# Attention scores with each head's block of q in its own quarter of the TensorE array

## The chip, the cores and the metric

One core of one Trainium2 chip. The metric is the device time of one execution, in microseconds; the median of the runs counts. The engines are called PE (TensorE matmuls; PEld its weight loads), DVE (VectorE), ACT (ScalarE), POOL (GpSimd) and SP (SyncE, which issues the transfers).

## The reference, cut to what matters

Attention for 2 batches of 8 heads, 768 positions, 64 values per head, float32. Every query sees the keys less than 16 positions away and, for each block of 32 positions, one pooled key (the maximum over the block) with a pooled value (the mean).

```
k_sum = k.reshape(B, H, nb, block, D).max(axis=3)
v_sum = v.reshape(B, H, nb, block, D).mean(axis=3)
scores_l = scale * np.matmul(q, k.transpose(0, 1, 3, 2))
mask_l = np.abs(pos[:, None] - pos[None, :]) < window
scores_s = scale * np.einsum('bhsd,bhnd->bhsn', q, k_sum) + np.log(block)
a = softmax(concatenate([where(mask_l, scores_l, -1e9), scores_s], -1))
out = np.matmul(a, np.concatenate([v, v_sum], axis=2))
```

The result, 1536 tokens of 512 values, goes through a mixture of 8 experts (router by argmax, 512 to 1024 to 512) and a dense feed-forward layer (512 to 2048 to 512, squared relu).

## The kernel before, in words

The heads are worked in 8 pairs (4 pairs for each batch); a pair's two heads lie one above the other on the 128 partitions, 64 each. A pair's 768 queries are 12 tiles of 64. For a tile, 96 keys around it and the 24 pooled keys, 120 in all, stand beside one another in `kt`. The array's stationary operand was built as a block-diagonal 128 x 128 matrix in `qb`: q of head 0 (64 x 64) in the upper left, q of head 1 in the lower right, zeros elsewhere. One matmul of `qb` with `kt` (128 x 120) so gives 128 rows of scores, 64 for each head. In float32 each matmul is two passes on PE, each with its weight load (96 matmuls stand as 192 in the profile).

Tiles go in groups of four (`groups`: 23 of four tiles and 2 of two at the end), and one iteration of the main loop (L569) issues a stage of several groups, so that each engine has its part of another group: `do_t(i-2)` transposes the weights of the group before the last (L383) and ACT copies them (L385); `do_s(i)` makes scores (L360) into a tile `ps` of one PSUM bank, and DVE adds the mask and takes the maximum (L366); `do_o(i-3)` multiplies with v (L401), DVE divides (L407); `prep(i+2)` lays out keys (POOL, L282), pooled keys (L284) and q (L287), mostly on ACT, for two groups ahead; `do_x(i-4)` transposes the result (L429); `do_l(i-5)` multiplies with the router's weights (L448); `do_e(i)` takes exp on ACT (L375). The order of all engines' instructions is that of the program text.

At every third iteration a new pair of heads begins. Then SP issues, one after another: the spreading of the pooled values into `vw` (`put_vsum`, L317), which waits for the small transfer `vt` (`vmean`, L314), and behind it the loads of k, q and v for pairs to come (L260, L261, L291, L294). `vmean(n+1)` is issued two iterations later, then `store_x` (L420). SP is one queue in order of issue.

At the end of the stage the first expert's weights are loaded, tokens are sorted by expert, and 13 slots of 128 tokens go through the experts; then comes the dense layer. These use hi and lo parts in float32r, three matmuls for each product. The change doesn't touch them.

Of the kernel before, what the change touches and what calls it, by code (L numbers as in the profile page):

```python
# [11 lines left out]
F32 = mybir.dt.float32  # L12
# [14 lines left out]
P = 128  # L27
NT = S // 64
# [12 lines left out]

# columns of the float32 constants
C_ID = 0
# [43 lines left out]
def tile_kernel(ctx: ExitStack, tc: tile.TileContext, a, out, dbg=None):  # L87
    nc = tc.nc
    ctx.enter_context(tc.manual_schedule())

    # ---- pools that live through the kernel
    cp = ctx.enter_context(tc.tile_pool(name="const", bufs=1))
# [17 lines left out]

    # ---- moe2 weights: float64 bits to float32
    pend, todo = [], [(j, c) for j in range(NF) for c in range(2)]
# [44 lines left out]

    # ---- a slot of 128 tokens of one expert
    def gather(s, x=None, rows=N):
# [59 lines left out]

    # ================= attention =================  # L220
    rt = ctx.enter_context(tc.tile_pool(name="route", bufs=1))
# [4 lines left out]
    with ExitStack() as ax:  # L226
# [14 lines left out]
        kts = [kq.tile([P, NT, NK], F32, name=f"kt{i}") for i in range(2)]  # L241
        qbs = [kq.tile([P, NT, P], F32, name=f"qb{i}") for i in range(2)]
        vws = [wk.tile([NK, NT, 129], F32, name=f"vw{i}", bufs=1) for i in range(3)]
        nc.gpsimd.memset(qbs[0], 0.0)
        for t in vws:
# [17 lines left out]
        STARTK = {0:nc.vector.tensor_copy,1:nc.vector.tensor_copy}  # L263
        STARTQ = {0:nc.vector.tensor_copy}

# [10 lines left out]
        def prep(i):  # L276
            n, t0, c = groups[i]
            kp, qp = kqs[n]
            kt, qb = kts[n % 2][:, t0:t0 + c], qbs[n % 2]
            w = kp[:, 64 * t0:64 * t0 + 96]  # L280
            w = bass.AP(w.tensor, w.offset, [list(w.ap[0]), [64, c], [1, 96]])
            nc.gpsimd.tensor_copy(kt[:, :, NB:], w)  # L282
            ek, *eq = (STARTK.get(i, nc.scalar.copy), STARTQ.get(i, nc.scalar.copy), nc.scalar.copy)
            ek(kt[:, :, 0:NB], kss[n].unsqueeze(1).broadcast_to([P, c, NB]))  # L284
            for h in range(2):
                r = slice(64 * h, 64 * h + 64)
                eq[h](qb[r, t0:t0 + c, r], qp[r, 64 * t0:64 * t0 + 64 * c].rearrange("p (t q) -> p t q", q=64))  # L287

# [6 lines left out]

        # means of v over the blocks: [block, quarter of the columns] on the partitions, then [block]
        def vsum(n, lo=0, hi=32):
# [22 lines left out]
        groups = [(n, t, 4) for n in range(8) for t in (0, 4, 8)][:-1] + [(7, 8, 2), (7, 10, 2)]  # L320
        # the tensor engine gets to its full clock
        zw = kq.tile([P, P], F32, name="zw")
        nc.vector.memset(zw, 0.0)
        nc.vector.memset(qbs[1], 0.0)
        warm = kq.tile([1, 1], F32, name="warm")
# [6 lines left out]
        kp, qp = kqs[0]  # L332
# [21 lines left out]
        def do_s(i):  # L354
            n, t0, c = groups[i]
            kt, qb = kts[n % 2], qbs[n % 2]
            pb = ps_s.tile([P, 512], F32, name="ps", tag="ps")
            ps = pb[:, 0:c * NK].rearrange("p (c k) -> p c k", k=NK)
            for u in range(c):
                nc.tensor.matmul(ps[:, u], qb[:, t0 + u], kt[:, t0 + u], start=True, stop=True)  # L360
            spare[i] = pb[:, 4 * NK:]
            sm = wk.tile([P, c, NK], F32, name="sm", tag="sm")
            mx = wk.tile([P, c], F32, name="mx", tag="mx")
            # the negated scaled scores, and the least of them
            for u in range(c):
                nc.vector.tensor_tensor_reduce(sm[:, u], ps[:, u], msk[:, (t0 + u > 0) + (t0 + u == NT - 1)], -0.125, 3e38,  # L366
                                               op0=ALU.add, op1=ALU.min, accum_out=mx[:, u:u + 1])
            sp[i] = sm, mx
# [94 lines left out]
        mxl = rt.tile([P, NTILE], F32, name="mxl")  # L463
        # of every token: experts as [taken | later than the taken], expert-major
        oh = rt.tile([P, B, 2, E, 6], F16, name="oh")
# [20 lines left out]

        # The first token's expert comes first. Its weights are loaded ahead, and its first 128 tokens
        # of the first batch are gathered before the second batch is through: beside column sums of
        # the scores (iterations 18 to 21).
        def first_slot(i, x):  # L490
# [7 lines left out]
            elif i == 20:  # L498
                mine = rsh[:, 0, 0, 0:1]
                nc.tensor.matmul(x[:, 0:1], ones, csh[:, C_NEG:C_NEG + 1], start=True, stop=False)  # L500
                nc.tensor.matmul(x[:, 0:1], tri, mine, start=False, stop=True)
                nc.tensor.matmul(x[:, 1:2], ones, mine, start=True, stop=True)

                def after():
                    r6 = vb.tile([P, 6], F16, name="r6", bufs=1)
                    nc.vector.tensor_scalar(r6, cum[:, 0, 0], x[:, 0:1], None, op0=ALU.add)
                    # what the first slot lacks, and where the second one begins
                    nc.vector.tensor_scalar(few, x[0:1, 1:2], P - 0.5, None, op0=ALU.is_lt)
                    nc.vector.tensor_scalar(row1, x[0:1, 1:2], float(P), None, op0=ALU.min)
                    nc.vector.tensor_scalar(lack[:, E:E + 1], x[0:1, 1:2], -float(P), 0.0, op0=ALU.add, op1=ALU.min)  # L510
                    nc.vector.tensor_scalar(lack[:, 0:1], lack[:, E:E + 1], -1.0, None, op0=ALU.mult)
                    nc.vector.tensor_tensor(t6, tok[:, 0:6], oh[:, 0, 0, 0], op=ALU.mult)
                    nc.vector.tensor_tensor(a6, io12[:, :, 0:6], r6.unsqueeze(1).broadcast_to([P, P, 6]), op=ALU.is_equal)
            elif i == 21:
                for d in range(6):
                    nc.tensor.matmul(x[:, 0:1], a6[:, :, d], t6[:, d:d + 1], start=d == 0, stop=d == 5)

                def after():
                    ixs[0] = rt.tile([P, 1], I32, name="ix0")
                    nc.vector.tensor_copy(ixs[0], x[:, 0:1])  # L520
                    gather(0, wk.tile([P, DM], F32, name="xg0", bufs=1), S)
            else:
                return None
# [173 lines left out]

    # ================= routing =================
    yp0 = ctx.enter_context(tc.tile_pool(name="yp0", bufs=1, **tiled))
# [20 lines left out]
    with ExitStack() as rx:  # L720
# [23 lines left out]

        # position of every token in the order by expert
        for b in range(B):
# [30 lines left out]
        nc.vector.tensor_scalar(nf, cb[:, 0:1], P + 0.5, None, op0=ALU.is_lt)  # L777
        # the second slot begins with the 129th token in the order, if the first slot is a full one
        ixs[1] = order_i[:, 1:2]
# [10 lines left out]
    def tables():  # L790
        s5 = [1, NREG, E]
        # slots of 128 tokens of one expert: expert of each
        ci = rg.tile([1, E], I32, name="ci")
# [10 lines left out]
        nc.vector.tensor_scalar(ec, er, float(E - 1), None, op0=ALU.min)  # L804
        # as it is numbered outside
        eo_ = rg.tile([1, NREG], F32, name="eo_")
# [5 lines left out]
        yield  # L812
        # first row of each slot; what lies past the last one goes to rows of its own
        off = rg.tile([1, E], F32, name="off")
# [11 lines left out]

        # gate of every token
        ex = rg.tile([P, NTILE, E], F32, name="ex")
# [15 lines left out]
    def w_split(j):  # L844
        wh = whs[j] = st.tile([P, 1024], F32R, name="st4", tag="st4") if j < 2 else w2p.tile([P, 1024], F32R, name=f"wh{j}", tag=f"wh{j}")
        nc.scalar.copy(wh, wf[j])
        # it takes the place of a chunk that is already split
        wl = wls[j] = wf_tile(F32R) if j <= NF else \
            w2p.tile([P, 1024], F32R, name="wf", tag="wf", bufs=NCH - NF)
        nc.vector.tensor_tensor(wl, wf[j], wh.bitcast(F32), op=ALU.subtract)  # L850

    # ================= mixture of experts =================
    with mx_:
# [76 lines left out]

        # dense rows that the first 11 and 12 slots have filled for good, however the tokens are spread:
        # at most 8 of them are not full
        def y_first_load(t):
# [65 lines left out]

    # ================= second feed-forward =================  # L1000
    with ExitStack() as fx:
# [8 lines left out]
        NI = NW * NCH  # L1010
        # relu(g a)^2 = g^2 relu(a)^2 as every gate is positive
        gd = yp.tile([P, NTILE], F32, name="gd")
# [23 lines left out]
        def z_mm(i):  # L1036
# [13 lines left out]
            if i == NI - LAST:  # L1050
                # the other window's tiles are read no more
                gh, gl = (t[:, 0] for t in yt1)
# [56 lines left out]
def lay_out(q, k, v, moe_modality_id, moe_w_gate, moe_modality_bias, moe_w1, moe_w2, moe2_w_in, moe2_w_out):  # L1109
    """The arrays as the program takes them: the inputs' own values, moved and padded."""  # L1110
    hp = H // 2
# [51 lines left out]
```

## Time and profile before

| | |
|---|---|
| runs | 569.95, 573.24, 574.92 us; median 573.24 |
| profiled execution | span 569.4 us from the first to the last instruction; its own time is not recorded apart, the lowest run is 0.5 us above the span |
| PE busy | 533.9 us (94%), 2676 matmul passes |
| PEld busy | 442.1 us (78%), 2676 weight loads |
| DVE, ACT, POOL busy | 293.1, 223.6, 100.7 us |
| granted PE clock | mean 0.972 of full |
| attention | about the first 105 us |

A busy engine is not an engine at its peak: matmuls are pipelined, and one instruction's duration is its latency, so the cost of a pass is read from the distance between starts. Idle time of an engine counts only where it is the one that the next step waits for.

### The profile page before, as it was taken

To read this page: it belongs to the slowest core of one execution; us is meant where nothing else is said; L and a number is where in the kernel's file an instruction comes from. 1 tells how busy PE (TensorE), PEld (TensorE's weight loads), DVE (VectorE), ACT (ScalarE), POOL (GpSimd) and SP (SyncE) were. 2 spreads that over 40 slices of the span, in tenths; PEclk is the share of its full clock that TensorE was granted. 3 is DMA by queue.
4 is the path that set the end of the run, shared out by engine and by line. 5 is a ranking of instruction groups with operands and counts; after the bars stand their busy time and mean duration, and the time that the engine had idled before them with its cause. 6 is when DMAs were issued, how large, how long until landed. Compare 5 with 4: busy or idle time off the path is not lost. (4 is left out here: it accounts for less than half of the span.)

```text
span 569.4 us, 8409 instructions
## 1 busy us (share of the span) xinstructions
PE 533.9 (94%) x2676; PEld 442.1 (78%) x2676; DVE 293.1 (51%) x836; ACT 223.6 (39%) x454; POOL 100.7 (18%) x115
## 2 busy tenths in 40 slices
PE   7795987979999999999889999999999999999995
PEld 6795976858878688888678888888888888888884
DVE  5885898571646953444968886423223223222230
ACT  5975886522225422223653445223222223221220
POOL 3333444640111500000317000002000000200002
PEclk8988899888999999999999999999999999999998
DMA  7795978603668644448519010001000000100001
GB/s 218 194 258 130 240 195 259 202 20 112 133 183 309 211 147 142 137 134 272 209 45 335 17 37 18 20 0 39 37 1 0 1 1 20 55 1 0 1 18 55
DMA packets 39829, 62.72 MB, mean 110 GB/s; under 512 B 19586, under 2 KB 22446, under 8 KB 39770
## 3 DMA queue, kind: packets, MB, share of 16 engines
q1 hardware_dynamic: 37386, 55.48, 32.6%
q0 software_dynamic: 2384, 6.56, 3.5%
q8 instruction: 23, 0.38, 0.3%
q14 instruction: 36, 0.29, 0.2%
HBM read 51.09 MB, written 9.71 MB: 107 GB/s over the span
## 5 line engine op out<-in xcount | busy, mean ns | idle before, releaser
L1049 DVE TENSOR_TENSOR g<-r 128x512 f32<-128x512 f32 x48 | 33.2, 691 | 106.0 <-ACT r L1047 106.0
L1047 ACT ACTIVATE r<-pz 128x512 f32<-128x512 f32 x48 | 28.7, 597 | 111.4 <-PE pz L1045 111.4
L1071 PE MATMUL pu<-wf,gh 128*128 128x512 f32 x180 | 70.5, 392 | 0.0
L1072 PE MATMUL pu<-wh,gl 128*128 128x512 f32 x156 | 61.6, 395 | 0.0
L1070 PE MATMUL pu<-wh,gh 128*128 128x512 f32 x156 | 61.5, 394 | 0.0
L1080 POOL DMA_INDIRECT out<-o,order_i x12 | 11.7, 976 | 236.8 <-DVE o L1079 215.4
L1044 PE MATMUL pz<-yt0h,wf 128*128 128x512 f32 x128 | 50.5, 395 | 0.0
L1058 ACT CAST gh<-g 128x512 fp32r<-128x512 f32 x45 | 28.0, 621 | 54.4 <-DVE g L1049 50.0
L1059 DVE TENSOR_TENSOR gl<-g,gh 128x512 fp32r<-128x512 f32 x45 | 31.2, 693 | 30.9 <-ACT gh L1058 28.9
L1043 PE MATMUL pz<-yt0h,wh 128*128 128x512 f32 x112 | 44.5, 397 | 0.0
L401 PE MATMUL po<-vw,pts 120*128 120x129 f32 x192 | 29.7, 297 | 15.4 <-DMA vw<-vt 10.8
L1045 PE MATMUL pz<-yt0l,wh 128*128 128x512 f32 x112 | 43.7, 390 | 0.0
L204 DVE TENSOR_TENSOR hl<-pt,hh 128x512 fp32r<-128x512 f32 x24 | 16.6, 690 | 47.7 <-ACTq L712 30.6
L177 PE MATMUL py<-w2l,hh 128*128 128x512 f32 x96 | 38.2, 398 | 2.9 <-DVE w2l L165 2.6
L178 PE MATMUL py<-w2h,hl 128*128 128x512 f32 x96 | 38.5, 401 | 1.6 <-DVE hl L204 1.4
L1071 PEld LDWEIGHTS pu<-wf,gh 128*128 128x128 f32 x180 | 33.8, 188 | 8.0
L401 PEld LDWEIGHTS po<-vw,pts 120*128 120x128 f32 x192 | 26.0, 206 | 17.8 <-issue 8.5
L176 PE MATMUL py<-w2h,hh 128*128 128x512 f32 x96 | 39.2, 409 | 0.0
L176 PE MATMUL ph<-w1h,xh 128*128 128x512 f32 x96 | 38.9, 405 | 0.0
L177 PE MATMUL ph<-w1l,xh 128*128 128x512 f32 x96 | 38.1, 397 | 0.0
L178 PE MATMUL ph<-w1h,xl 128*128 128x512 f32 x96 | 37.9, 395 | 0.0
L1072 PEld LDWEIGHTS pu<-wh,gl 128*128 128x128 f32 x156 | 29.3, 188 | 7.0
(239 smaller groups left out, 1129.5 us busy)
## 6 DMA issues: line engine op xcount, KB each, us to landing
st<-in_w SPq DMA_DIRECT2D x24, 512.0 KB
rw<-in_w SPq DMA_DIRECT2D x16, 512.0 KB
wf<-in_w SPq DMA_DIRECT2D x8, 512.0 KB
wh<-in_w SPq DMA_DIRECT2D x8, 512.0 KB
vw<-in_vw SPq DMA_DIRECT2D x7, 580.5 KB
y_dram<-ys SPq DMA_DIRECT2D x13, 256.0 KB
vk<-in_vk SPq DMA_DIRECT2D x8, 384.0 KB
wf<-in_kt SPq DMA_DIRECT2D x7, 400.0 KB
```

Source lines behind the costliest of these rows:

```text
L176: nc.tensor.matmul(ps, ah, bh, start=first, stop=False)
L177: nc.tensor.matmul(ps, ah, bl, start=False, stop=False)
L178: nc.tensor.matmul(ps, al, bh, start=False, stop=last)
L401: nc.tensor.matmul(po[-1][:, v, 0:129], pts[:, u + v], vw[:, t0 + u + v], start=True, stop=True)
L1043: nc.tensor.matmul(pz, wh[:, c], yh[:, k], start=k == 0, stop=False)
L1044: nc.tensor.matmul(pz, wl[:, c], yh[:, k], start=False, stop=False)
L1045: nc.tensor.matmul(pz, wh[:, c], yl[:, k], start=False, stop=k == 3)
L1049: nc.vector.tensor_tensor(g, r, r, op=ALU.mult)
L1059: nc.vector.tensor_tensor(gl, g, gh.bitcast(F32), op=ALU.subtract)
L1070: nc.tensor.matmul(acc[t], gh[:, c], wh, start=j == 0, stop=False)
L1071: nc.tensor.matmul(acc[t], gh[:, c], wl, start=False, stop=False)
L1072: nc.tensor.matmul(acc[t], gl[:, c], wh, start=False, stop=j == NCH - 1)
```

## The change

`qb` goes: its two buffers, their two memsets and the copies in `prep`. `do_s` takes q where the transfer has put it. Head h's 64 x 64 block of q is loaded as the stationary operand into the rows 64h to 64h+63 and the columns 64h to 64h+63 of the array, and multiplies only that head's half of `kt`. A tile's scores come from two matmuls where there was one; they land in the same places of the same PSUM tile.

```
-        qbs = [kq.tile([P, NT, P], F32, name=f"qb{i}") for i in range(2)]
-        nc.gpsimd.memset(qbs[0], 0.0)
...
-        STARTQ = {0:nc.vector.tensor_copy}
...
         def prep(i):
             n, t0, c = groups[i]
-            kp, qp = kqs[n]
-            kt, qb = kts[n % 2][:, t0:t0 + c], qbs[n % 2]
+            kp = kqs[n][0]
+            kt = kts[n % 2][:, t0:t0 + c]
...
-            ek, *eq = (STARTK.get(i, nc.scalar.copy), STARTQ.get(i, nc.scalar.copy), nc.scalar.copy)
+            ek = STARTK.get(i, nc.scalar.copy)
             ek(kt[:, :, 0:NB], kss[n].unsqueeze(1).broadcast_to([P, c, NB]))
-            for h in range(2):
-                r = slice(64 * h, 64 * h + 64)
-                eq[h](qb[r, t0:t0 + c, r], qp[r, 64 * t0:64 * t0 + 64 * c].rearrange("p (t q) -> p t q", q=64))
...
-        nc.vector.memset(qbs[1], 0.0)
...
         def do_s(i):
             n, t0, c = groups[i]
-            kt, qb = kts[n % 2], qbs[n % 2]
+            kt, qp = kts[n % 2], kqs[n][1]
             pb = ps_s.tile([P, 512], F32, name="ps", tag="ps")
             ps = pb[:, 0:c * NK].rearrange("p (c k) -> p c k", k=NK)
             for u in range(c):
-                nc.tensor.matmul(ps[:, u], qb[:, t0 + u], kt[:, t0 + u], start=True, stop=True)
+                for h in range(2):
+                    r = slice(64 * h, 64 * h + 64)
+                    nc.tensor.matmul(ps[r, u], qp[r, 64 * (t0 + u):64 * (t0 + u) + 64], kt[r, t0 + u], start=True, stop=True)
```

## Rows read from the trace of the kernel before

**Rows 1.** The page: busy tenths of PE in 40 slices of the span.

```profile
PE   7795987979999999999889999999999999999995
```

**Rows 2.** Windows: busy us (and instructions) of each engine in 20 us stretches.

```profile
core 0: us, PE busy (x) PEld busy (x) DVE busy (x) ACT busy (x) POOL busy (x), PEclk, DMA share, GB/s
...
40.00:60.00 20.00, 14.23 (x101) 13.82 (x101) 11.60 (x63) 12.14 (x37) 5.73 (x10) 0.83 0.66 165
60.00:80.00 20.00, 19.04 (x167) 18.50 (x167) 17.66 (x106) 17.23 (x52) 7.46 (x15) 1.00 0.86 234
```

**Rows 3.** Timeline, one dense group: start, length in all, what, how many.

```profile
65.10 1.05 PE L360 MATMUL ps<-kt,qb 128*128 128x120 f32 x8
...
65.99 1.06 PE L401 MATMUL po<-vw,pts 120*128 120x129 f32 x8
...
66.30 0.56 ACT L385 COPY pts<-pt 120x512 f32<-120x512 f32 x1
...
67.11 0.51 PE L448 MATMUL pl<-wg,xt 128*128 128x16 f32 x4
...
67.94 1.05 PE L360 MATMUL ps<-kt,qb 128*128 128x120 f32 x8
...
69.34 0.56 ACT L385 COPY pts<-pt 120x512 f32<-120x512 f32 x1
```

**Rows 4.** Waits of PE and PEld, 14 to 97 us: total us, times, longest.

```profile
PE po L401 <- DMA vw<-vt: 8.1, 4, 5.5
...
PEld po L401 <- ACT p L375: 4.6, 6, 1.6
PEld po L401 <- ACT qb L287: 2.6, 2, 1.9
```

**Rows 5.** Timeline of SP's transfers, and of PE at the stage's end.

```profile
34.38 0.84 SPq L317 DMA_DIRECT2D vw<-vt  x1
...
39.85 0.83 SPq L314 DMA_DIRECT2D vt<-vs  x1
...
50.64 0.84 SPq L317 DMA_DIRECT2D vw<-vt  x1
...
96.85 0.84 SPq L317 DMA_DIRECT2D vw<-vt  x1
...
100.28 1.41 PE L401 MATMUL po<-vw,pts 120*128 120x129 f32 x8 [2.65 <-DMA vw<-vt]
```

**Rows 6.** Groups by line and shape: busy us, mean ns, idle before.

```profile
L287 ACT COPY qb<-wf 64x256 f32<-64x256 f32 x45 | 18.1, 403 | 6.1 <-DMA wf<-in_qt 5.8
...
L448 PEld LDWEIGHTS pl<-wg,xt 128*64 128x64 f32 x8 | 0.6, 136 | 0.6 <-issue 0.6
```

**Rows 7.** Timeline, the second group at the start.

```profile
8.46 0.82 ACT L287 COPY qb<-wf 64x256 f32<-64x256 f32 x2 [2.83 <-DMA wf<-in_qt]
...
11.45 0.28 DVE L366 CUSTOM_DVE_ANT_0 sm<-ps,cst 128x120 f32<-128x120 f32 x1 [1.44 <-PE ps L360]
```

**Rows 8.** Timeline of PE and PEld, router products with whole and half weights.

```profile
108.63 0.27 PE L429 MATMUL px<-cst,xo 128*128 128x128 f32 x1
...
109.65 0.39 PE L178 MATMUL pt<-w1h,xl 128*128 128x512 f32 x1
109.88 0.27 PE L429 MATMUL px<-cst,xo 128*128 128x128 f32 x1
...
110.99 0.39 PE L178 MATMUL pt<-w1h,xl 128*128 128x512 f32 x1
...
108.63 0.53 PEld L448 LDWEIGHTS pl<-wg,xt 128*128 128x128 f32 x4
...
110.08 0.31 PEld L448 LDWEIGHTS pl<-wg,xt 128*64 128x64 f32 x4 [0.28 <-issue]
```

**Rows 9.** Timeline of PE around the 12-row matmul L451.

```profile
60.98 0.52 PE L448 MATMUL pl<-wg,xt 128*128 128x16 f32 x4
61.43 0.42 PE L451 MATMUL pl<-mb,m 12*128 12x48 f32 x2
...
62.26 1.05 PE L360 MATMUL ps<-kt,qb 128*128 128x120 f32 x8
```

## The prediction

> **What bounds the kernel now.** First the page's slices: TensorE (PE) is near full from slice 11 on and gappy only in the first seven or eight, which are the attention stage [rows 1]. Behind that stage PE runs without gaps, so I take it that a shift of the end of attention shows one for one at the end of the kernel. Next the windows: between 60 and 80 us PE works 19.04 of 20 us and ScalarE (ACT) 17.23, between 40 and 60 us PE only 14.23 [rows 2]. So the stage has two faces, dense groups and groups that wait.
>
> The timeline of one dense group shows the first. Scores start at 65.10 and again at 67.94: 2.84 us per group of four tiles. The eight score passes take 65.10 to 65.99, 0.111 us each. ACT meanwhile runs from one copy of the transposed weights to the next, 66.30 to 69.34, that is 3.04 us, without a gap [rows 3]. PE and ACT are both at their limit there, ACT a little over.
>
> The list of waits shows the second face. From 14 to 97 us the product with v (L401) waits 8.1 us for the DMA that spreads the block means of v, and its weight loads wait 4.6 us for exp and 2.6 us for the qb copies on ACT [rows 4]. The first of these belongs to a loop on the DMA queue: the means of head pair n+1 leave at L314 behind the bulk loads that follow L317 of pair n, and L317 of pair n+1 waits until they land. The one issued at 39.85 let L317 go at 50.64; four pairs later L317 is at 96.85, so a head pair there takes (96.85 - 50.64)/4 = 11.55 us, against 3 x 2.84 = 8.52 us of dense PE work. The last of them is what L401 waits for at 100.28, the end of the stage [rows 5]. So attention is paced by DMA round trips with some 3.0 us of PE slack per head pair, and by PE and ACT only between two such waits.
>
> **The change part by part.** *Removed.* ACT loses 49 qb copies (45 of them 403 ns [rows 6], the four of the last two groups shorter, two to a group), about 0.81 us per full group: its 3.04 us become 2.23, and ACT stops being a limit. One such copy leaves VectorE and two memsets go at the start, where their engines wait for data anyway; I count these at nothing, and without that cover they would be a gain of the same small size. The score matmul now waits for q's DMA itself instead of for a copy of it. In the loop no group could start earlier than that DMA before either, so this adds no wait; only SyncE's loads stand behind it and nobody's order changes.
>
> *The start.* The second group's q is copied from 8.46 on, PE starts its scores after that, and VectorE waits 1.44 us for them until 11.45 [rows 7]. Without the two copies (0.82 us) scores can start as the DMA lands. Gain 0 to 0.9 us; at most, since the block means and q's own DMA come next. I take 0.8.
>
> *Added: more passes.* A float32 matmul is two passes, each a weight load and a stream. Per group 8 passes with 128 columns of weights become 16 with 64. What does a 64-column load cost? The router product L448 does exactly that in its last two groups: four loads of 64 columns span 0.31 us [rows 8] at a mean of 0.136 [rows 6], so they follow at (0.31 - 0.136)/3 = 0.058 us, where four of 128 columns span 0.53 [rows 8]. Sixteen at 0.058 make 0.93 us against 0.89 now. The streams: four router passes of 16 columns span 0.52 us [rows 9], eight score passes of 120 columns 1.05 [rows 3]; less the pitch of 0.111, one lasts 0.187 and 0.273, so 104 more columns cost 0.086 and 120 columns about 0.10 us (an estimate from these rows). No row shows two quarters of the array at work together. The lower bound is that the second head's passes run beside the first's: 16 x 0.10 / 2 = 0.80, under the 0.93 of the loads. The upper is that they follow one another: 1.60. I take 0.93, since in every row here streams and loads overlap freely and the two quarters share neither rows nor columns.
>
> *Added: changing between whole array and quarters,* twice a group (after the transposes at L383, before L401). Two places of the trace show such a round trip. From the transpose at 108.63 to the one at 109.88 lie one transpose, four whole router passes and three long matmuls: 1.25 us. From 109.88 the same with four 64-column passes ends at 110.99 + 0.23 = 111.22 (0.23 as from 109.65 to 109.88): 1.34, although the passes themselves should be 4 x (0.111 - 0.058) = 0.21 shorter. Round trip 0.30 us [rows 8]. The 12-row matmul L451 slips two passes (0.22) in between router and scores: 60.98 to 62.26 is 1.28 us [rows 9] against 67.11 to 67.94, 0.83 [rows 3]: round trip 0.23. I take 0.26, with 0.23 and 0.30 as ends.
>
> *Sum on PE.* 0.93 - 0.89 + 0.26 = +0.30 us per group, so a dense group is 3.14 us of PE where it was 2.84 of PE and 3.04 of ACT; 24 groups' worth is 7.2 us of PE work (6.5 to 8.2).
>
> *What of it reaches the end.* Three groups make 9.42 us, still under the 11.55 of the DMA loop, so the waits for the block means (8.1 us, and 2.65 at 100.28) take most of it up. They can't take up what delays the loop itself: the block means leave late where computing made them late, as at 39.85, 5.5 us after the L317 of the pair before at 34.38; there are two such places in the loop [rows 5]. Between the wait that releases PE and such a point lie about 2.3 groups: 2 x 2.3 x 0.30 = 1.4 us. Against it stand the 0.8 of the start. The ACT waits (4.6 + 2.6 us) vanish, but they lie in stretches that end at a DMA wait; I count them at nothing net, and at most at their whole 7.2. Sum: +1.4 - 0.8 = +0.6 us. On the profiled span, 569.4, that is 570.0; the median of the runs, 573.24, is 3.8 us above that span, and I forecast from the median: 574. Bounds of this case: nothing is absorbed, +7.2 (580.4), or half of the ACT waits count, -3.0 (570).
>
> **The rivals.** *The quarters take turns (slower).* Both heads' scores of a tile go to one PSUM bank, in different partitions. If PE can't run the two together, 1.60 us replace 0.93 and a group costs 0.97 more: 3.81, or 11.43 per head pair. That is the point from which it decides: it fills the DMA loop's 11.55, so every point at which computing feeds the loop is late. 24 x 0.97 = 23 us of PE work, less the 8.1 + 2.65 us of waits that it can fill, leaves about 12; with the start and the lost ACT waits I say +9, or 582 (577 to 587). For it: no row shows two quarters at once. Against: they differ in rows, columns and PSUM partitions. That no quarter is formed at all, and each pass runs as a narrow one on the whole array, belongs here: no round trip, but the same turns, 0.71 per group.
>
> A rule that speaks for this rival is in the Trainium skill, TensorEngine Tiling (Array Packing), Restrictions and Gotchas: different row tiles can't access one PSUM bank at the same time. By that rule the time would be this rival's; no run shown here has two row tiles, so the trace neither agrees nor disagrees. The same page, Key Properties, has tiles load and multiply independently, which would be my forecast.
>
> *ACT was the real brake (faster).* ACT is busy through every dense group, and PE's waits on it come up between the DMA waits. If these 7.2 us are on the path that feeds the block means, as VectorE's order behind exp suggests, the stage loses 7.2 + 0.8 and gains 1.4: -6.6, or 566.5. For it: ACT's 3.04 exceed PE's 2.84. Against: the largest waits are for DMA, and PE's new 3.14 exceeds the old 3.04.
>
> **How the numbers follow.** Forecast (quarters together, mostly absorbed) 0.55, taking turns 0.27, ACT the brake 0.18. One per cent is 5.7 us, about what the runs, 5 us apart, can tell from none. Slower by over 1% (above 579): most of the second case, 0.24, and 0.04 of the first. Faster (under 567.5): two thirds of the third case, 0.12, and 0.04 of the first, which runs' scatter allows. Within: 0.56. The range leaves out a tenth on either side: 566 to 584.
>
> **What the new profile would show.** Right: L287 gone, ACT idle some 0.8 us in each dense group; score passes with 64 x 64 weights, 16 per group within about 0.9 to 1.0 us, starts in pairs; the first L401 behind them some 0.1 us late; dense groups 3.1 to 3.2 us apart; L317 of the last pair within 2 us of 96.85. Taking turns would show as passes 0.10 apart throughout, groups 3.8 us apart, and few waits for the block means. I am wrong if the clock also falls to its lower level in attention more often than now, if the round trip costs well over 0.30, or if L317 moves by more than PE's own delay.

## The result

| kernel | median (lowest to highest), us | executions | profiled: span, mean granted clock |
|---|---|---|---|
| before | 572.07 (568.13 to 574.95) | 20 | 569.4 us, 0.972 |
| after | 576.98 (572.76 to 581.03) | 20 | 572.4 us, 0.963 |

The ratio is 1.0071, with an interval of 1.005 to 1.0093: slower by 4.9 us. The time lies inside the forecast range, 3 us above the forecast. The two profiled executions differ by 3.0 us, so the traces below can account for 3.0 of the 4.9 us. Ratios leave out slow executions, which matter in one kernel below (*turns*: 6 of 13, five of them at about 600 us and the profiled one among these), where the time given leaves them out too.

**Attention after the change.** In the kernel after, the lines behind `do_s` have numbers lower by 4: scores L356, transposes L379, product with v L397. First the page's slices (compare PE with [rows 1]; PEclk is the granted clock):

```profile
PE   7797998979999999999879999999999999999995
...
PEclk7978699979999999999989999999999999999999
```

PE is a little fuller early on, and the stage ends where it did. Slice 21 (286 to 300 us) stands at 7 where it stood at 8; that place comes below. The timeline of one dense group (start, length in all, engine, line, what, how many), PE first, then PEld, then ACT, as in [rows 3]:

```profile
67.59 0.63 PE L379 MATMUL pt<-cst,p 128*120 128x128 f32 x4
68.15 1.04 PE L356 MATMUL ps<-kt,wf 64*64 64x120 f32 x16
69.11 1.16 PE L397 MATMUL po<-vw,pts 120*128 120x129 f32 x8
70.11 0.38 PE L425 MATMUL px<-cst,xo 128*128 128x128 f32 x2
...
71.26 1.04 PE L356 MATMUL ps<-kt,wf 64*64 64x120 f32 x16
...
68.14 0.81 PEld L356 LDWEIGHTS ps<-kt,wf 64*64 64x64 f32 x16 [0.17 <-issue]
...
68.90 0.57 ACT L381 COPY pts<-pt 120x512 f32<-120x512 f32 x1
...
70.58 0.37 ACT L427 COPY xt<-px 128x256 f32<-128x256 f32 x1 [0.95 <-PE px L425]
...
72.01 0.57 ACT L381 COPY pts<-pt 120x512 f32<-120x512 f32 x1
```

Scores start at 68.15 and again at 71.26: 3.11 us per group against 2.84, +0.27 where +0.30 was forecast. The scores take 69.11 - 68.15 = 0.96 us until the next operation starts, against 0.89. Sixteen passes last 1.04 us in all; with the 0.273 of one pass that makes (1.04 - 0.273)/15 = 0.051 from pass to pass in the mean. They start in pairs, though, one pass of each head: in narrow windows at 68.20, 68.33 and 68.43 us the same timeline shows two, four and six of them.

```profile
68.15 0.32 PE L356 MATMUL ps<-kt,wf 64*64 64x120 f32 x2
68.15 0.42 PE L356 MATMUL ps<-kt,wf 64*64 64x120 f32 x4
68.15 0.53 PE L356 MATMUL ps<-kt,wf 64*64 64x120 f32 x6
```

From pair to pair it is 0.10 to 0.11 us, so one head's passes stand 0.10 apart and the other head's run beside them. ACT has 0.95 us of idle time in each group, and its period is now PE's (72.01 - 68.90 = 3.11).

What paces the stage, from the same view at the start, at the last transfer of block means, behind it, and at the first product behind the routing (the last line is of the kernel before):

```profile
10.70 0.28 DVE L362 CUSTOM_DVE_ANT_0 sm<-ps,cst 128x120 f32<-128x120 f32 x1 [0.47 <-PE ps L356]
...
95.93 0.84 SPq L311 DMA_DIRECT2D vw<-vt  x1
...
100.66 1.21 PE L397 MATMUL po<-vw,pts 120*128 120x129 f32 x8 [0.88 <-ACT pts L381]
...
121.31 1.03 PE L767 MATMUL pall<-bm,rw 128*128 128x12 f16 x12 [2.93 <-DVE rw L764]
...
120.90 1.03 PE L771 MATMUL pall<-bm,rw 128*128 128x12 f16 x12 [2.89 <-DVE rw L768]
```

VectorE has the second group's scores at 10.70 where it was 11.45 [rows 7]. The last transfer starts at 95.93 where it was 96.85 [rows 5]. The product that waited 2.65 us for it [rows 5] now waits 0.88 for ACT's copy of the transposed weights. The first product behind the routing starts at 121.31; in the kernel before it was 120.90. So in these two executions attention gave 0.4 us away, about as forecast, and most of the 4.9 us has to come from elsewhere.

**Where the time went.** The experts' matmuls end and the dense layer begins at 291 us. Between them stands the branch over the code of the overflow slots (`with tc.If(...)` in `more`, L983 before, L979 after), which this input never enters: every engine jumps over that code. PE's timeline there, first of the kernel before:

```profile
291.18 0.40 PE L178 MATMUL py<-w2h,hl 128*128 128x512 f32 x1
292.94 0.47 PE L1043 MATMUL pz<-yt0h,st 128*128 128x512 f32 x1 [1.36 <-PEq L983]
```

and of the kernel after, with ACT's next instruction:

```profile
290.86 0.40 PE L178 MATMUL py<-w2h,hl 128*128 128x512 f32 x1
294.26 0.50 PE L1039 MATMUL pz<-yt0h,st 128*128 128x512 f32 x1 [3.00 <-ACTq L979]
...
295.15 0.63 PE L1039 MATMUL pz<-yt0h,st 128*128 128x512 f32 x1
295.58 0.63 PE L1040 MATMUL pz<-yt0h,wf 128*128 128x512 f32 x1
...
304.28 0.39 PE L1066 MATMUL pu<-st,gh 128*128 128x512 f32 x1
...
294.45 1.05 ACT L842 CAST wh<-wf 128x1024 fp32r<-128x1024 f32 x1 [2.57 <-ACTq L979]
```

PE waited 1.36 us for its own sequencer; now it waits 3.00 for ACT's, at the line of the branch. Right after it the matmuls follow one another at 0.43 instead of 0.23 us. The windows say why (busy us and instructions of PE, PEld, DVE, ACT and POOL, then the granted clock, the DMA share and GB/s):

```profile
292.00:296.00 4.00, 1.74 (x5) 1.37 (x6) 1.03 (x2) 1.05 (x1) 0.96 (x1) 0.87 0.23 80
296.00:300.00 4.00, 4.00 (x14) 3.23 (x13) 1.06 (x2) 0.60 (x1) 3.17 (x3) 0.71 0.61 184
```

In the kernel before the clock is 1.00 in both windows and PE runs 19 passes in the second; here it falls to its lower level (a granted 0.50, 1.2 of 2.4 GHz) for 3.4 us after PE stood still, and 14 passes fit. The next product, `pu`, starts at 304.28; before it started at 301.36. So the 2.9 us are: last expert product 0.32 us earlier, wait 1.64 longer, and the remaining 1.6 us in the stretch of half clock. That is nearly all of the 3.0 us that the two spans differ by.

### The profile page after: what moved, and what is told of

The parts are those of the page before. It is cut to its first block, busy times and chain, and to the rows that moved or that the text cites. A ratio compares the mean times of both kernels' runs of the same rounds, so it can differ in the third digit from the quotient of the medians.

```text
span 572.4 us, 8745 instructions
## 1 busy us (share of the span) xinstructions
PE 541.4 (95%) x2868; PEld 441.8 (77%) x2868; DVE 291.5 (51%) x834; ACT 204.5 (36%) x405; POOL 100.9 (18%) x114
## 5 line engine op out<-in xcount | busy, mean ns | idle before, releaser
L397 PE MATMUL po<-vw,pts 120*128 120x129 f32 x192 | 31.8, 311 | 10.5 <-DMA vw<-vt 6.7
L177 PE MATMUL py<-w2l,hh 128*128 128x512 f32 x96 | 38.2, 398 | 2.7 <-DVE w2l L165 2.6
L397 PEld LDWEIGHTS po<-vw,pts 120*128 120x128 f32 x192 | 26.6, 211 | 15.2 <-issue 8.7
L177 PE MATMUL ph<-w1l,xh 128*128 128x512 f32 x96 | 38.1, 397 | 0.0
```

The lines of the kernel that those rows point to most:

```text
L177: nc.tensor.matmul(ps, ah, bl, start=False, stop=False)
L397: nc.tensor.matmul(po[-1][:, v, 0:129], pts[:, u + v], vw[:, t0 + u + v], start=True, stop=True)
```

## The experiments

Three theories. Q: the quarters cost in attention what the prediction summed up or more, and the kernel is slower for that. F: the loss is made at the jump over the unused code, where ACT's code behind the jump arrives late. D: attention is paced by its DMA loop, so a few tenths of a us per group, on PE or on ACT, don't reach the end. Each kernel was timed in five rounds against the kernel before on the same chip, whose median was 571.5 to 571.9 us; the numbers behind a time are its ratio to that and the interval. Three chips were used (experiments 1 to 4; 5 to 7 and 12; 8 to 11), so a distance between two of these kernels is good to some 2.5 us.

**1 and 2. Both kernels without the jump.** The code for overflow slots is left out; for this input it does nothing.

```diff
-        more(SLOTS0)
```

> The changed kernel without the code for a 14th and later slot of tokens, which this input never enters (left out: that code and the branch over it). Theory F, code loading: the 3 us that the changed kernel lost in the profiled run come from ScalarE's instructions behind that branch, which are loaded only after the jump; PE waits for them 3.00 us instead of 1.36 and then runs 3.4 us at the lower clock. Without the branch PE's wait before the dense layer is under 1 us, no lower clock follows, and the kernel takes 571 to 573. Theory Q, the quarters themselves: the loss lies in attention, and this kernel takes 575 to 577.

> The kernel before, with the same code and branch left out. Theory F: it gains only the 1.36 us of its own wait, 570 to 572, so the distance to the changed kernel without the branch shrinks from 4 to 0.5 to 1.5 us. Theory Q: the distance stays at 4 us or more.

After without the jump: 570.33 us, 0.9986 (0.9953 to 1.0018). Before without it: 570.31, 0.9988 (0.9958 to 1.0019). The distance of 4.9 us is gone, as far as the two intervals (each some 1.8 us to either side) can tell. The only wait of PE that is left between 280 and 300 us is one of 2.6 us for VectorE (L177) that both kernels have with the jump too.

Q falls: with the same 16 passes and both switches per group, no loss against the kernel with the copies can be measured. The loss is made where the jump is, and F is left.

**3. The kernel after, with copies in place of ACT's lost instructions.** 48 copies of one element, unread: 24 at the start, two in each of twelve slots. That was meant to bring ACT's program ahead of the branch back to its old length.

```diff
+        for _ in range(24):
+            nc.scalar.copy(warm, zw[0:1, 0:1])
...
+                for _ in range(2):
+                    nc.scalar.copy(pad, regs[:, 0, 0:1])
```

> The changed kernel with 48 one-element copies on ScalarE (24 at the start, 2 in each of 12 slots), as many instructions as ScalarE has lost ahead of the branch. Theory F: the place of ScalarE's code is as in the kernel before, PE's wait at the dense layer is 1.4 us and the time 573 to 574. Theory Q: 577, the wait anything.

574.5 us, 1.005 (1.0025 to 1.0075), and the wait did not go:

```profile
PE pz L1045 <- ACTq L985: 3.8, 1, 3.8
```

The place is F's, the expectation was a miss. But the edit did not do what it was meant to. Of the kernel after and of this run, one line's semaphore instructions on ACT:

```profile
L192 ACTq EVENT_SEMAPHORE  x24: 17/17/2464, 110.6 to 279.9; - x24
...
L192 ACTq EVENT_SEMAPHORE  x3: 17/17/2461, 111.6 to 139.7; - x3
```

With the 48 copies 33 semaphore instructions went, 21 of them here. Counted in the traces, ACT has 612 instructions ahead of the branch in the kernel before, 564 in the kernel after and 579 in this one. So this run does not say whether the old length would have given the time back.

**4. The kernel before, with a longer way to jump.** 128 copies inside the skipped code; none is executed.

```diff
                 more(s + 1)
+                if s == SLOTS0:
+                    for _ in range(128):
+                        nc.scalar.copy(pad, regs[:, 0, 0:1])
```

> The kernel before with 128 one-element copies on ScalarE inside the code that is jumped over, none of them executed. Theory F: the target of the jump lies further off and has to be loaded after the jump, PE waits about 3 us and falls to the lower clock: 574 to 576. Theory Q: no change, 572.

575.31 us, 1.0074 (1.0047 to 1.0101): the kernel before gets as slow as the kernel after (1.0071) by instructions that never run. PE's timeline, and the windows behind it:

```profile
295.53 0.79 PE L1047 MATMUL pz<-yt0h,st 128*128 128x512 f32 x1 [3.15 <-ACTq L984]
```

```profile
296.00:300.00 4.00, 4.00 (x11) 3.03 (x11) 0.97 (x1) 1.04 (x1) 2.85 (x3) 0.50 0.36 115
300.00:304.00 4.00, 4.00 (x16) 3.22 (x15) 1.64 (x3) 2.04 (x3) 2.94 (x4) 0.82 0.81 262
```

The same wait for ACT's sequencer, and the lower clock behind it, here for longer. This is the run that decides for F: besides the 128 instructions only a tile of one element, for them to write, was added.

The Trainium skill, Runtime: NRT & Kernel Launch, Instruction fetch mechanics, says that prefetch is sequential and that a taken branch whose target isn't loaded must fetch it before the engine goes on. By that rule a longer jump on ACT alone delays ACT behind it, and this run agrees: PE now waits for ACT, 3.15 us, where it waited 1.36 for its own sequencer.

**5 and 6. The kernel after, with a shorter way.** In the first only one overflow slot's code is kept; in the second all of it, but its weight copies are written for GpSimd, so that ACT has less to jump over.

```diff
         def more(s):
-            if s == SLOTS:
+            if s == SLOTS0 + 1:
                 return
```

```diff
-                fill(s, 1, (0, 1, 2, 3))
+                fill(s, 1, (0, 1, 2, 3), nc.gpsimd.tensor_copy)
...
-                fill(s, 2, (0, 1, 2, 3))
+                fill(s, 2, (0, 1, 2, 3), nc.gpsimd.tensor_copy)
```

> The changed kernel with code for one overflow slot instead of seven (the other six, which this input never enters, are left out): ScalarE's jump skips 23 rows of the program instead of 119. Theory F, code loading: the branch is still there, but its target is near, in code that is already loaded; PE waits about 1 us before the dense layer, and the time is 570 to 573. If it is the branch itself, at any distance, that costs: 575 to 577.

> The changed kernel, whole, with the eight weight copies of each overflow slot written for GpSimd instead of ScalarE (this input never executes them): ScalarE's jump skips 63 rows instead of 119. Theory F: if the target then lies in loaded code, PE's wait falls to about 1 us and the time is 571 to 573; if a block boundary still lies between, 575 to 577 as before.

The first: 573.08 us, 1.0019 (0.9986 to 1.0052). The second: 572.72, 1.0000 (0.9969 to 1.0032). PE's waits at the jump, of the first and of the second:

```profile
PE pz L1039 <- ACTq L979: 0.9, 1, 0.9
```

```profile
PE pz L1039 <- PEq L979: 1.3, 1, 1.3
```

3.00 becomes 0.9 and 1.3, and the kernel with the quarters is level with the kernel before. In the second nothing of the executed work differs from the kernel after; only ACT's skipped code is shorter, and GpSimd's longer.

**7. The kernel before with that shorter way** (the same edit as the second above).

> The kernel before, whole, with the same overflow copies written for GpSimd. Theory F: no more than its own wait of 1.36 us to gain, 570 to 572; within 1.5 us of the changed kernel with the same edit, if that one's target is loaded.

571.69 us, 0.9998 (0.9975 to 1.002). It had nothing to gain there: PE waits 1.6 us for its own sequencer, as before.

The trace also records ACT's branch itself and its next instruction, a semaphore. From the start of the one to the start of the other it took, in us:

| before | after | after_pad | before_far | after_short | after_light | before_light | experiment 12 |
|---|---|---|---|---|---|---|---|
| 0.43 | 2.27 | 3.34 | 2.70 | 0.17 | 0.17 | 0.42 | 0.43 |

The three kernels in which this time is over 2 us are the three that are slower than the kernel before by 0.5 to 0.74%; the other four with a jump can't be told from it.

The trace shows code being loaded, too: the profile counts packets of instruction queues, without saying for which engine. Those of one queue (packets, MB, share) between 285 and 300 us, in the kernel after and in the same kernel without the jump:

```profile
q14 instruction: 6, 0.05, 1.3%
...
q14 instruction: 1, 0.01, 0.2%
```

The kernel before has 7 there, and none without the jump. In the kernel before ACT's next instruction starts at 292.39 us, ahead of the first of these packets behind ACT's branch (292.98); in the kernel after it starts at 294.19, 1.07 us after the first two have landed (293.12). The other kernels of the table divide in the same way: in the three with over 2 us such packets land before ACT goes on, in the others none has started by then.

**8. The quarters in turns.** The kernel after without the jump, with the two heads one behind the other, so that eight passes in a row use one quarter.

```diff
-            for u in range(c):
-
-                for h in range(2):
+            for h in range(2):
+                for u in range(c):
```

> The changed kernel without the branch, but in each group the first head's four quarters come before the second head's four, so that neighbouring passes use the same quarter and must take turns. If the two quarters of a tile really ran side by side, these passes now stand 0.10 us apart instead of 0.05, the sixteen take 1.6 us, dense groups are 3.8 us apart, and the kernel loses 5 to 12 us against the 570.3 of the changed kernel without the branch: 575 to 582. If it was the order of loads that gave the pace and not two quarters at once, nothing changes: 570.

575.85 us (the median of the seven executions that count), 1.0068 (1.0032 to 1.0103), 5.5 us above the same kernel with alternating heads. A dense group at full clock, and below it three narrow windows of its scores (at 37.20, 37.43 and 37.98 us):

```profile
37.16 1.50 PE L355 MATMUL ps<-kt,wf 64*64 64x120 f32 x16
38.59 1.16 PE L396 MATMUL po<-vw,pts 120*128 120x129 f32 x8
...
40.73 1.50 PE L355 MATMUL ps<-kt,wf 64*64 64x120 f32 x16
...
37.16 0.31 PE L355 MATMUL ps<-kt,wf 64*64 64x120 f32 x1
37.16 0.52 PE L355 MATMUL ps<-kt,wf 64*64 64x120 f32 x3
37.73 0.53 PE L355 MATMUL ps<-kt,wf 64*64 64x120 f32 x6
```

The scores take 1.43 us, and groups are 3.57 apart (forecast for this rival: 3.81). The mean from pass to pass is (1.50 - 0.273)/15 = 0.082 us, but it is a mix. Within the first head a pass starts every 0.10 us, one at a time, as the forecast's estimate had it; in the middle six start within 0.27 us, because the second head's first passes already run beside the first head's last. So this kernel takes turns only in part, and its loss needn't be all that full turns would cost. That alternating heads run side by side is what the pairs of the kernel after show, and this run shows what it is worth.

The rule from the Trainium skill that spoke for this rival (TensorEngine Tiling (Array Packing), Restrictions and Gotchas: row tiles can't access one PSUM bank at once) is not borne out here. Both heads write one bank, in different partitions, and their passes start in pairs 0.10 us apart, which is the time of one head's pass alone; the measurement decides.

**9. Only the change between whole array and quarters.** The kernel before without the jump, with one 64 x 64 product of one column behind each group's scores; its result is not read.

```diff
                 nc.tensor.matmul(ps[:, u], qb[:, t0 + u], kt[:, t0 + u], start=True, stop=True)
+            nc.tensor.matmul(pb[0:64, 510:511], qb[0:64, t0, 0:64], kt[0:64, t0, 0:1], start=True, stop=True)
```

> The kernel before without the branch, with one 64x64 product of one column added behind each group's scores (into columns of the bank that nobody reads): the change to quarters and back, 0.27 us, and two short passes, and nothing else. Theory D: the 24 x 0.35 = 8 us of TensorE work are mostly taken up by waits for transfers, 570 to 573. If TensorE paces attention: 576 to 578.

```profile
76.61 1.05 PE L360 MATMUL ps<-kt,qb 128*128 128x120 f32 x8
77.59 0.27 PE L361 MATMUL ps<-kt,qb 64*64 64x1 f32 x2
...
79.84 1.05 PE L360 MATMUL ps<-kt,qb 128*128 128x120 f32 x8
```

A group is 3.23 us, 0.39 more than in [rows 3], for two passes and both switches. Over 24 groups that is 9.4 us of PE work. The time is 572.33 us, 1.0 (0.9969 to 1.0032): 2.0 us above the kernel before without the jump. So most of the nine us are absorbed, seven by the medians and about five at the least within the intervals: D.

**10. The copies of q left where they were, unread.** The kernel after without the jump, with ACT's qb copies back.

```diff
+            for h in range(2):
+                r = slice(64 * h, 64 * h + 64)
+                nc.scalar.copy(qb[r, t0:t0 + c, r], qp[r, 64 * t0:64 * t0 + 64 * c].rearrange("p (t q) -> p t q", q=64))
```

> The changed kernel without the branch, with the copies of q into the block-diagonal tile put back on ScalarE, though nobody reads them: quarters without the relief of ScalarE. Theory D: 570 to 572. If relief and slower TensorE cancelled each other in the changed kernel: 574 to 577, and q_on_pool gains as much.

570.98 us, 0.9995 (0.997 to 1.002), 0.65 above the same kernel without them, which is less than the runs can tell. So ACT's relief and the slower PE don't cancel each other, which would have made it 574 to 577. ACT is as full as in the kernel before; its timeline:

```profile
68.85 0.56 ACT L386 COPY pts<-pt 120x512 f32<-120x512 f32 x1
...
69.49 0.82 ACT L286 COPY qb<-wf 64x256 f32<-64x256 f32 x2
...
71.96 0.56 ACT L386 COPY pts<-pt 120x512 f32<-120x512 f32 x1
```

**11 and 12. The copies of q on GpSimd.** The kernel before without the jump, and then with the whole jump over the lightened code of 6.

```diff
-            ek, *eq = (STARTK.get(i, nc.scalar.copy), STARTQ.get(i, nc.scalar.copy), nc.scalar.copy)
+            ek, *eq = (STARTK.get(i, nc.scalar.copy), STARTQ.get(i, nc.gpsimd.tensor_copy), nc.gpsimd.tensor_copy)
```

> The kernel before without the branch, with the copies of q on GpSimd instead of ScalarE (one stays on VectorE): ScalarE is relieved as by the change, and TensorE keeps its whole-array passes. Theory D, attention is paced by transfers: 569 to 571, no gain to be measured. Theory S, ScalarE was a brake: 564 to 567. GpSimd has some 0.35 us for such a copy, two to a group, and may itself come late behind its waits for transfers.

> The kernel before, whole, with the copies of q on GpSimd and the overflow copies written for GpSimd: a version that might beat both. Theory F and D: 569 to 571, as without the branch; if ScalarE's code, shorter by the copies of q, lands in a block that isn't loaded, 573 to 576.

Without the jump 569.18 us, 0.9954 (0.9928 to 0.9979). That is clear of the kernel before, but part of it is the jump that is gone: the kernel before without the jump (experiment 2) is 1.1 us above it, with overlapping intervals. As a whole kernel 572.78, 1.0008 (0.9978 to 1.0039). ACT's relief without the quarters is worth 1.1 us by the medians and some 4 at the most, and no whole kernel here is measurably faster than the kernel before. Between 14 and 97 us PE waits longer for the block means than in [rows 4], and not at all for a copy of q:

```profile
PE po L401 <- DMA vw<-vt: 11.6, 4, 4.8
```

## Why the prediction was right, and where it was not

*The start* was right: 0.8 us forecast, 0.75 measured (10.70 for 11.45). It doesn't reach the block means: their first transfer leaves at 10.25 us, before at 10.04.

*More passes.* Forecast 0.93 us of scores for 0.89, because loads set the pace at 0.058. The mechanism was right in what mattered (both heads together, starts in pairs, no turns), and the limit was the other one: eight pairs at 0.10 are about 0.82 us, which is the forecast's lower bound from its estimate of 0.10 for a stream of 120 columns. The sixteen loads span 0.81 us, paced like the passes.

*The round trip.* Forecast 0.26 (0.23 to 0.30). From the transposes to the scores it is 68.15 - 67.59 = 0.56 us, before 0.46; the scores take 0.96, of which the pairs explain about 0.82; from L397 to the next L425 it is 1.00, before 0.90. So the two changes cost about 0.10 + 0.14 + 0.10 = 0.34 us, and the passes gain 0.07 (0.82 for 0.89). Together that is the 0.27 per group. The forecast's sum of +0.30 is near it because two terms were off in opposite ways (scores +0.04 for -0.07, round trip 0.26 for 0.34), which is luck. The experiment with a single small product pays 0.39 for the same and its two passes.

*What of it reaches the end.* Forecast +1.4 - 0.8 = +0.6 us by the end of attention; measured +0.4 at the first product behind the routing, and 0.0 between the medians of the two kernels without the jump, good to some 2.5 us. Experiment 9 shows the absorption by itself: 9.4 us of PE work in, 2.0 out. The +1.4 itself is not borne out. It counted two places where computing makes the block means late; in the kernel before there are three where they leave 5.4 us or more after the L317 of the pair before (39.85, 66.34, 89.46). And it let each delay through whole. What SP waited for between 30 and 100 us, first before, then after:

```profile
SPq L317 <- DMA vt<-vs: 31.0, 6, 8.5
SPq L314 <- DVE mx L366: 6.3, 3, 2.6
...
SPq L311 <- DMA vt<-vs: 19.7, 6, 7.0
SPq L308 <- DVE mx L362: 12.9, 3, 5.0
```

SP's wait for computing, before it could send the block means, doubled (6.3 to 12.9 us), but its wait for them to land got shorter by more (31.0 to 19.7), and the last transfer left 0.9 us earlier, not later, inside the 2 us allowed. So in these two executions the loop had room at this point as well.

One of the signs that were to make me wrong did come, by these two executions: the granted clock was lower in attention. But the kernel before without the jump, which has the same attention as the kernel before, is as low, so the sign is not shown to come from the quarters. Windows of before, before_nojump and after:

```profile
14.00:97.00 83.00, 69.56 (x552) 66.59 (x551) 65.93 (x357) 63.90 (x193) 30.74 (x53) 0.93 0.80 217
14.00:97.00 83.00, 70.62 (x535) 68.27 (x535) 62.57 (x346) 62.61 (x190) 27.76 (x51) 0.87 0.80 214
14.00:97.00 83.00, 73.96 (x698) 65.17 (x696) 63.09 (x346) 44.79 (x144) 28.71 (x51) 0.87 0.81 216
```

*ACT as the brake* was rightly the smaller case: with its 0.8 us per group back, the median moves by 0.65 us (experiment 10). (By its own terms its sum was 566.6, not 566.5.)

*Taking turns* was priced at +9 us; made on purpose, and only in part, it cost 5.5.

*The step that failed* is "Behind that stage PE runs without gaps, so I take it that a shift of the end of attention shows one for one at the end of the kernel", and with it the removal of 49 copies from ACT's program, which the prediction costed by their busy time alone. There is a gap at 291 us, 1.36 us of waiting for a sequencer. [rows 1] had a sign of it that was passed over: slices 20 and 21 (270 to 299 us) stand at 8 among nines. In the kernel after the wait is 3.00, and the stretch of lower clock behind it cost about as much again as the wait grew. The forecast was 0.8 us above the median of the kernel before, the result is 4.9 above it. The 4.1 us between them are made at this place: they go with the jump, though the traces show only 3.0 of the 4.9. That the time lies in the range is luck: the range was made wide for other things that could go wrong.

*What is shown of the cause, and what is not.* Shown: without the jump the two kernels can't be told apart; lengthening ACT's skipped code alone makes the kernel before slow at the same place by the same wait; shortening it brings the kernel after back; instruction packets move right behind the jump, and ACT goes on after them in the slower kernels and ahead of them in the others. The sizes can fit, as an estimate: 1.64 us of wait, and 1.6 us for a lower clock that lasts 3.4 us, so twice that where it lasts 6.8 as in experiment 4; together 3.2 to 4.8 of the 4.9 us. The one trace of the kernel after has the shorter stretch. Open: what put the kernel after on the far side. Its ACT program has 48 instructions less ahead of the branch (49 copies less, one semaphore instruction more), and where the branch and its target then lie is the argued cause. The skipped part is equally long in both kernels, so it has to be the position or the moment. Experiment 3 doesn't settle it, since it left the program 33 instructions short, and ACT's step over the branch got longer still (3.34 us for 2.27). The trace doesn't show which engine a packet of code is for.

## What to carry over

Where a kernel jumps over unused code, price that jump as a place of its own: look at what each engine waits for right behind it, since instructions added to code that never runs moved this kernel by 0.74%, and an edit far ahead of the jump went along with as much (0.71%). Test such a suspicion by removing the branch in both kernels before explaining a small difference by the edit itself. Two 64 x 64 quarters on the diagonal do work side by side if their passes alternate, but for these float32 scores that only about makes up for the doubled number of passes (0.82 us for 0.89), and each stay in quarters costs some 0.3 us. A mean over a row of passes hides how they lie: look at narrow windows before saying what runs beside what.

## Unexpected on the chip

128 instructions that never run, on one engine, cost 0.7% of a kernel of 570 us: 3.15 us of waiting and then the lower clock.

The granted clock can stay at its lower level although PE never stops. In the profiled execution of *turns* PE is busy for the whole of this window, and the granted clock is 0.50. What keeps it there is not shown.

```profile
60.00:80.00 20.00, 20.00 (x102) 17.95 (x102) 8.31 (x45) 6.96 (x22) 8.23 (x15) 0.50 0.76 194
```
